# Attention and SwiGLU block: the last exponentials and masks of batch 0, and the order of tile 1's output pieces

## The chip, the core and the metric

The kernel runs on one core of a Trainium2 chip. The core has TensorE (PE, matrix products into PSUM), VectorE (DVE), ScalarE (ACT), GpSimd (POOL) and SyncE (SP); each works through its own instructions in order, and they wait for one another through semaphores. The metric is the device time of one execution in microseconds (us). Seven runs of the kernel before gave 240.5 to 241.52 us, with a median of 241.03 us. One execution was also recorded by the profiler, and all times inside the kernel are of that one, counted from the start of its span.

## What is computed

The reference is an attention with a few global keys and a local window, followed by a gated feed-forward block:

```python
scores = scale * np.matmul(q, k.transpose(0, 1, 3, 2))   # (4, 8, 768, 64): batch, heads, sequence, head width
keep = is_global | is_local            # 8 global keys, a window of 96 keys
bias = -slopes[:, None, None] * dist[None, :, :]
scores = np.where(keep, scores + bias[None], -1e9)
a = np.exp(scores - max); a = a / (sum(a) + 1e-9)
attn = np.matmul(a, v)                 # to rows of 512: heads side by side
g = x @ w_gate                         # 512 -> 1536
out = ((g * sigmoid(g)) * (x @ w_val)) @ w_out      # 1536 -> 512
```

There are 3072 rows (4 batches of 768) and the output is 3072 x 512 in float32.

## The kernel before

**Tiles.** The rows are cut into 8 tiles of 384. Tiles 0 and 1 are the two halves of batch 0, tiles 2 and 3 those of batch 1, and so on. The feed-forward of a tile `t` runs over 12 blocks `f` of 128 hidden columns. A block is a gate product `gps` and a value product `vps` (line 560, 4 matmuls of 384 columns each, in one PSUM bank each); then a tanh on ScalarE (`th`, line 571), and on VectorE `sl` (line 576, reads `th` and the gate bank) and `hT` (line 580, reads the value bank and `sl`). A gate bank comes free when `sl` is done, a value bank when `hT` is.

**Banks.** PSUM has 8 banks here: four that rotate for the attention (`a0` to `a3`), three that rotate for the products (`x0` to `x2`), and `o0`. In the blocks spoken of here, gate 7, value 7 and gate 8 of tile 0 take the three product banks in turn, and gate 9 takes that of gate 7 again. From `late_widen` until `narrow` (block 2 of tile 1) the products rotate over seven banks.

**Output pieces.** The output of 128 rows of a tile is a sum over the 12 blocks of the hidden layer, cut into 4 pieces of 3 matmuls (`out_part`, line 592, 512 columns), here called piece 0 to piece 3. All pieces add into the one bank `o0`; after piece 3 ScalarE copies it out (`osb`, line 598) and SyncE's queue stores it, and piece 0 of the next 128 rows can't begin before that copy is done. Pieces 0 to 3 read the four parts of the output weights `wo` (3 blocks each), which GpSimd's queue loads one after another.

**Attention of batch 0.** The heads go in four pairs. For the second half of batch 0 (rows of tile 1), `sch(hp)` issues the scores of pair `hp` in two parts, called which 0 and which 1. A part needs an `exps` (two activations on ScalarE, line 367) and a `mask` (multiplications by a table on VectorE, line 373: two for part 0, one of 864 columns for part 1). `vas(0, 1)` then sums the denominators (`den`) and the weighted values (`num`) of all pairs on TensorE (line 452). The denominators of the second four heads read part 1 of pair 3 near their end. After that VectorE inverts and spreads the denominators and writes the rows of tile 1 (`xT`).

**Order.** The order on every engine is the order of the program text. Work put off is appended to the list `later`, and `run_later(n)` takes the next n from it. The list `tile0` gives the order for tile 0: a pair `(f, 0)` is the gate of block f with its tanh and `sl`, `(f, 1)` the value with its `hT`. Ahead of most items one step of `later` is taken. The list `stretches` gives for each block of the later tiles how many output pieces follow it (`n_out`), with one step of `later` ahead of each piece; the attention steps of batch 1 are hung on blocks of tile 1 (`first(1, 1)`: transposes after blocks 2 and 5, scores after 4, 6 and 8, values after 9 and inside 10). `outs` is the list of all pieces in order; its first 12 are those of tile 0's three groups of 128 rows.

Before the change, pair 3's `later` holds exps of part 1, mask of part 0, mask of part 1, in this order. Nothing is taken ahead of `(7, 0)`; the exponentials are taken ahead of `(7, 1)`, the first mask ahead of `(8, 0)` and the second ahead of `(9, 0)`. Of tile 0's output pieces, two are issued at the end of `tile0`; tile 1's blocks 0 to 11 are followed by 0, 0, 0, 1, 2, 2, 1, 1, 1, 0, 2, 2.

Of the kernel before, what the change touches and what calls it, by code (L numbers as in the profile page):

```python
# [37 lines left out]
def kernel(  # L38
# [193 lines left out]
    def bank(name, dt=FP32):  # L232
        tag = state["tags"][state["n"] % len(state["tags"])]
        state["n"] += 1
        return single(name, tag, dt)

    def banks(name, dt=FP32):
        return [bank(name, dt) for _ in range(2)]
# [16 lines left out]
    def run_later(n):  # L255
        for _ in range(n):
            if later:
                later.pop(0)()
# [306 lines left out]
    def gate_or_val(t, f, which, c0=0):  # L565
        products(t, f, which, c0, NC)
        dst = gv.pop((f, which))

        if which == 0:
            th = sb2.tile([128, TB], FP32, name="th", tag="th")  # L570
            nc.scalar.activation(out=th, in_=dst[:, 0:TB], func=AF.Tanh, scale=0.5)  # L571
            if t == 0 and f < 4:
                sl = sb2.tile([128, TB], FP32, name="sl", tag="ns", bufs=4)
            else:
                sl = sb2.tile([128, TB], FP32, name="sl", tag="sl", bufs=3)
            nc.vector.scalar_tensor_tensor(  # L576
                out=sl, in0=th, scalar=1.0, in1=dst[:, 0:TB], op0=AluOp.add, op1=AluOp.mult)
            gv["sl", f] = sl
        else:
            nc.vector.tensor_mul(hTs[t][:, f, :], dst[:, 0:TB], gv.pop(("sl", f)))  # L580
# [143 lines left out]
    def sc(b, *units):  # L724
        def step():
            for i, (hp, bk, *other) in enumerate(units):
                pair = pairs[b + 1 if other else b, hp]
                on_vector = pair.b < 2 or bk < 2 or hp % 2 == 0
                exps, mask = pair.scores(
                    bk, nc.vector if on_vector else nc.gpsimd,  # L730
                    [spare("sc") for _ in range(2)] if i == 0 and len(units) == 3
                    else banks("sc"))
                if i == 0:
                    exps()
                else:
                    later.append(exps)
                later.append(mask)
        return step

    def va(b, g, half):  # L740
        return lambda: quads[b, g].values(half, bank, nc.vector)

    def vas(b, half):
        return lambda: both_values(b, half)

    def tr(b, hp):
        return pairs[b, hp].transposes
# [15 lines left out]
    def sch(hp):  # L763
        def step():
            p = pairs[0, hp]
            for which in range(2):
                p.scores_half(1, which, banks("sc"), which == 1 and hp != 1, True)
            if hp != 1:
                later.insert(0, later.pop(1))
        return step  # L770

# [8 lines left out]
    def first(t, b):  # L780
        return {(t, 2): [tr(b, 0), tr(b, 1)],
                (t, 4): [sc(b, (0, 0), (0, 1), (1, 0))],
                (t, 5): [tr(b, 2), tr(b, 3)],
                (t, 6): [sc(b, (1, 1), (2, 0), (2, 1))],
                (t, 8): [sc(b, (3, 0), (3, 1))],
                (t, 9): [va(b, 0, 0)],
                (t, 10, 1): [va(b, 1, 0), lambda: run_later(len(later))]}

    def both(t, b):

        n = b + 1
        return {(t, 0): [sc(b, (0, 2), (1, 2), (2, 2)), fetch(n, 0, 1)],
                (t, 5): [sc(b, (3, 2), (0, 0, n), (1, 0, n)), fetch(n, 2, 3)],
                (t, 8): [vas(b, 1)],
                (t + 1, 0): [sc(n, (0, 1), (1, 1), (2, 0))],
                (t + 1, 4): [sc(n, (2, 1), (3, 0), (3, 1))],
                (t + 1, 8): [vas(n, 0)]}
# [24 lines left out]
    def out_next():  # L822
# [3 lines left out]
             bias_of(0, 0), bias_of(0, 1), scores_of(0), (0, 1), (1, 1), (2, 1),  # L826
             trh(2, 3, False), sch(1), (3, 1), (4, 0), (5, 0), sch(2), (6, 0), (4, 1), (5, 1),
             (6, 1), sch(3), (7, 0), (7, 1), (8, 0), (9, 0), vas(0, 1), late_widen, (10, 0), (8, 1),
             (11, 0), (9, 1), (10, 1), out_next, (11, 1), out_next]

    def ff(t, f0, f1, n_out=(0,)):
        return [(t, f, n_out[(f - f0) % len(n_out)]) for f in range(f0, f1)]

    stretches = [
        (ff(1, 0, 6, (0, 0, 0, 1, 2, 2)) + ff(1, 6, 10, (1, 1, 1, 0)) + ff(1, 10, 12, (2,)), first(1, 1)),
        (ff(2, 0, 12, (1,)) + ff(3, 0, 12, (1,)), both(2, 1)),
        (ff(4, 0, 12, (1,)) + ff(5, 0, 12, (1,)), both(4, 2)),
        (ff(6, 0, 12, (1,)), second(6, 3)),
# [48 lines left out]
    for item in tile0:  # L887
        if callable(item):
            if item is not late_widen and item is not out_next:
                run_later(len(later))  # L890
            item()
            continue
        f, which = item
        if item == (8, 1):
            run_later(3)
        elif item not in ((6, 0), (7, 0)):
            run_later(1)
        gate_or_val(0, f, which, (NC if f < 4 else 0, 2 if f < 2 else 0)[which])
        for fn in after.pop((0, f, which), []):
            fn()  # L900
# [61 lines left out]
```

## Time and profile before

| | |
|---|---|
| median of 7 runs | 241.03 us |
| the profiled execution | 240.69 us |
| its span, first instruction to last | 238.8 us |
| VectorE busy | 170.0 us (71%) |
| ScalarE busy | 127.5 us (53%) |
| GpSimd busy | 94.1 us (39%) |
| granted TensorE clock, mean | 0.998 |

The span is the stretch that the trace covers; 1.89 us of the profiled execution lie outside it. The busy time of TensorE is a union of modelled spans: a matmul of 384 columns shows about 326 ns from start to end, while in an undisturbed row the next one starts 162.5 ns after it. So waits of TensorE are read from start to start, against 162.5 ns after a matmul of 384 columns and 216 ns after one of 512. Between about 50 us and the end, no such step in the trace is longer than its neighbours by more than the 0.05 to 0.1 us that come with a change of the kind of matmul.

### The profile page before, as it was taken

Reading aid. Unit: us, or ns where it says so; the run is one execution under the profiler, and the core shown is the slowest. Engines: PE = TensorE matmul, PEld = TensorE weight load, DVE = VectorE, ACT = ScalarE, POOL = GpSimd, SP = SyncE. Lnnn points to the kernel's source line nnn. Section 1 sums busy time; section 2 is a strip of 40 time slices with the busy share of each in tenths; the row PEclk is TensorE's granted clock in tenths of the full one; section 3 lists DMA queues with packets and bytes.
Section 4 is the critical chain, followed back from the end, with each engine's and each line's share of the span. In section 5 each row is a group of like instructions: output and inputs, shape, how many; then the busy total and the mean of one; then the engine's idle time right before and its main releaser. Section 6 shows DMA issues by size and latency. Waiting matters only on the chain.

```text
span 238.8 us, 6012 instructions
## 1 busy us (share of the span) xinstructions
PE 231.9 (97%) x2406; PEld 133.9 (56%) x2406; DVE 170.0 (71%) x372; ACT 127.5 (53%) x290; POOL 94.1 (39%) x113
## 2 busy tenths in 40 slices
PE   7899989989999999999999999999999999999994
PEld 4565565646555556555655556555655566555543
DVE  6879989948896678675885668676785668555530
ACT  4887774668847275367346365367356535233311
POOL 8976565578960003994082063700032213000000
PEclk9999999999999999999999999999999999999999
DMA  6999999999999447999039449920110110111022
GB/s 133 164 199 200 188 197 204 196 168 164 157 131 143 110 113 91 125 139 124 31 60 113 113 111 132 128 54 6 40 47 0 47 44 3 45 47 44 7 83 88
DMA packets 83332, 25.00 MB, mean 105 GB/s; under 512 B 72600, under 2 KB 80360, under 8 KB 83304
## 3 DMA queue, kind: packets, MB, share of 16 engines
q0 software_dynamic: 64208, 14.05, 66.2%
q1 hardware_dynamic: 18664, 10.36, 17.5%
q8 instruction: 19, 0.31, 0.5%
q10 hardware_dynamic: 432, 0.21, 0.4%
q14 instruction: 9, 0.07, 0.1%
HBM read 28.62 MB, written 6.29 MB: 146 GB/s over the span
## 4 chain that ended last, share of the span: by engine, by line
PE 91%; DVE 3%; DMA 2%; POOL 1%; ACT 1%; issue 1%; DVEq 0%; ACTq 0%; POOLq 0%
PE gps L560 26%; PE vps L560 26%; PE ops L592 25%; PE num L452 4%; PE sc L392 3%; DMA q<-in_q_dram 2%; PE den L452 2%; PE trs L272 1%; PE ops L608 1%; DVE sl L576 1%; PE sc L356 1%; PE sc L345 1%; POOL k L118 1%; DVE xT L510 1%; ACT th L571 1%; PE trs L298 1%
## 5 line engine op out<-in xcount | busy, mean ns | idle before, releaser
L571 ACT ACTIVATE th<-gps 128x384 f32<-128x384 f32 x96 | 47.3, 494 | 60.9 <-PE gps L560 56.5
L560 PE MATMUL gps<-xT,wg 128*128 128x384 f16 x384 | 77.8, 327 | 0.3 <-DVE xT L510 0.3
L576 DVE SCALAR_TENSOR_TENSOR sl<-th,gps 128x384 f32<-128x384 f32 x96 | 52.6, 551 | 35.6 <-ACT th L571 34.8
L560 PE MATMUL vps<-xT,wv 128*128 128x384 f16 x384 | 77.6, 326 | 0.0
L592 PE MATMUL ops<-wo,hT 128*128 128x512 f16 x276 | 73.1, 379 | 0.7 <-ACT osb L598 0.7
L580 DVE TENSOR_TENSOR hT<-vps,sl 128x384 f16<-128x384 f32 x96 | 52.8, 553 | 7.5 <-PE vps L560 0.2
L560 PEld LDWEIGHTS <-wg 128*128 128x128 f16 x384 | 35.4, 98 | 31.6 <-issue 2.2
L560 PEld LDWEIGHTS <-wv 128*128 128x128 f16 x384 | 37.2, 98 | 25.5 <-DMA wv<-in_moe_w_val_dram 0.3
L592 PEld LDWEIGHTS <-hT 128*128 128x128 f16 x276 | 26.9, 98 | 24.8 <-issue 1.2
L400 ACT ACTIVATE at<-sc 128x432 f16<-128x432 f32 x72 | 33.8, 534 | 11.0 <-PE sc L392 11.0
L529 POOL TENSOR_TENSOR xT<-ns,rb 128x384 f16<-128x384 f32 x10 | 9.8, 996 | 65.1 <-ACT ns L525 33.8
L169 POOL DMA_DIRECT2D vS<-in_v_dram x28 | 24.7, 892 | 5.4 <-DMA kst<-in_k_dram 1.6
L598 ACT ACTIVATE osb<-ops 128x512 f32<-128x512 f32 x23 | 13.7, 597 | 15.1 <-PE ops L592 14.9
L411 DVE TENSOR_TENSOR at<-at,masks 128x864 f16<-128x864 f16 x20 | 12.2, 609 | 7.1 <-ACT at L400 7.1
L411 POOL TENSOR_TENSOR at<-at,masks 128x864 f16<-128x864 f16 x4 | 7.3, 1821 | 23.9 <-ACT at L400 19.3
L525 ACT COPY ns<-num 128x384 f32<-128x384 f32 x24 | 9.8, 494 | 10.8 <-PE num L452 10.8
L192 POOL DMA_DIRECT2D kst<-in_k_dram x16 | 14.1, 896 | 1.8 <-PE sc L392 1.3
L192 POOL DMA_DIRECT2D qst<-in_q_dram x16 | 13.7, 880 | 0.7 <-issue 0.5
L367 ACT ACTIVATE at<-sc 128x432 f16<-128x432 f32 (+2 forms) x32 | 11.5, 461 | 1.7 <-PE sc L356 1.7
L408 DVE TENSOR_TENSOR at<-at,masks 128x432 f16<-128x432 f16 x24 | 8.1, 377 | 4.4 <-ACT at L400 4.4
L452 PE MATMUL num<-at,vS 128*32 128x216 f16 (+6 forms) x576 | 11.0, 224 | 0.0
L462 DVE STREAM_TRANSPOSE dT<-den 128x384 f32<-128x384 f32 x16 | 9.3, 580 | 1.1 <-PE den L452 0.4
(72 smaller groups left out, 166.0 us busy)
## 6 DMA issues: line engine op xcount, KB each, us to landing
out_dram<-osb SPq DMA_DIRECT2D x23, 256.0 KB
vS<-in_v_dram POOLq DMA_DIRECT2D x24, 120.0 KB, 5.6
wg<-in_moe_w_gate_dram POOLq DMA_DIRECT2D x6, 256.0 KB, 8.9
wv<-in_moe_w_val_dram POOLq DMA_DIRECT2D x6, 256.0 KB, 8.0
wo<-in_moe_w_out_dram POOLq DMA_DIRECT2D x4, 384.0 KB, 11.2
qst<-in_q_dram POOLq DMA_DIRECT2D x16, 96.0 KB, 4.7
kst<-in_k_dram POOLq DMA_DIRECT2D x16, 90.0 KB, 4.5
kst<-in_k_dram POOLq DMA_DIRECT2D x2, 384.0 KB, 11.7
```

What stands on the lines that cost most here:

```text
L169: nc.gpsimd.dma_start(out=vSs[b][NG:NG + n, c, :, :], in_=v[b, :, KC * c:KC * c + n, :].rearrange("h p d -> p h d"))
L192: nc.gpsimd.dma_start(out=st[b][p0:p0 + n, h // 2, :, h % 2, :], in_=src[b, h, 0:n * J].rearrange("(t p) d -> p t d", p=n))
L367: nc.scalar.activation(out=at[:, hi, 0:col + n], in_=sc[hi][:, 0:col + n], func=AF.Exp, scale=scale)
L400: nc.scalar.activation(out=at[:, hi, :], in_=sc[hi][:, 0:BANK], func=AF.Exp, scale=scale)
L411: mul_eng.tensor_mul(at, at, m[:, :, o:o + BANK])
L452: nc.tensor.matmul(dst[r, o:o + n], lhsT=ones[:, 0:32] if side is None else vals[:, 4 * g + j, side::2], rhs=pairs[b, 2 * g + j // 2].at[c ...
L560: nc.tensor.matmul(gv[f, which][:, 0:TB], lhsT=w[:, c, 128 * f:128 * f + 128], rhs=x_of(t)[:, c, :], start=(c == 0), stop=(c == NC - 1))
L571: nc.scalar.activation(out=th, in_=dst[:, 0:TB], func=AF.Tanh, scale=0.5)
L576: nc.vector.scalar_tensor_tensor(out=sl, in0=th, scalar=1.0, in1=dst[:, 0:TB], op0=AluOp.add, op1=AluOp.mult)
L580: nc.vector.tensor_mul(hTs[t][:, f, :], dst[:, 0:TB], gv.pop(("sl", f)))
L592: nc.tensor.matmul(ops, lhsT=hTs[t][:, f, 128 * i:128 * i + 128], rhs=wo[:, f, :], start=(f == 0), stop=(f == NFF - 1))
L598: nc.scalar.mul(out=osb, in_=ops, mul=0.5)
```

## The change

```diff
@@ sch(hp) @@
             for which in range(2):
-                p.scores_half(1, which, banks("sc"), which == 1 and hp != 1, True)
-            if hp != 1:
+                p.scores_half(1, which, banks("sc"), which == 1 and hp == 2, True)
+            if hp == 2:
                 later.insert(0, later.pop(1))
@@ tile0 @@
-             (11, 0), (9, 1), (10, 1), out_next, (11, 1), out_next]
+             (11, 0), (9, 1), (10, 1), out_next, (11, 1)]
@@ stretches @@
-        (ff(1, 0, 6, (0, 0, 0, 1, 2, 2)) + ff(1, 6, 10, (1, 1, 1, 0)) + ff(1, 10, 12, (2,)), first(1, 1)),
+        (ff(1, 0, 6, (1, 0, 0, 1, 1, 2)) + ff(1, 6, 10, (1,)) + ff(1, 10, 12, (2,)), first(1, 1)),
@@ loop over tile0 @@
         if item == (8, 1):
             run_later(3)
-        elif item not in ((6, 0), (7, 0)):
+        elif item != (6, 0):
             run_later(1)
```

With it, pair 3's exponentials of part 1 are issued at once behind those of part 0, ahead of the tanh of block 7; its mask of part 0 is taken ahead of `(7, 0)` and its mask of part 1 ahead of `(7, 1)`. Pairs 1 and 2 keep their order. Of the two pieces at the end of `tile0` the second is issued after block 0 of tile 1; one of the two after block 4 moves back, so that block 4 has one, and block 9 has one where it had none. Tile 1's blocks are followed by 1, 0, 0, 1, 1, 2, 1, 1, 1, 1, 2, 2. The sum of pieces from the end of `tile0` to block 11 is 14 in both, and from block 10 on each place has the same piece as before. No instruction is added or removed, and nothing computed is changed.

## The prediction

> **What bounds the kernel.** TensorE does. I read the page's busy line first, then the waits from 29 us on with TensorE alone, then the chain of waits, and last the timelines of the three engines around each place, with the starts of single instructions.
>
> ```profile
> PE 231.9 (97%) x2406; PEld 133.9 (56%) x2406; DVE 170.0 (71%) x372; ACT 127.5 (53%) x290; POOL 94.1 (39%) x113
> ```
> ```profile
> PE ops L592 <- ACT osb L598: 0.7, 1, 0.7
> PE den L452 <- DVE at L373: 0.6, 1, 0.6
> ```
>
> Two waits are left, both where the change works. From start to start they are longer than the view says, since it counts from a modelled end. In the denominators one matmul starts at 31.885 and the next at 32.762; such neighbours follow within 0.003, so **0.874 us** are lost. Between piece 3 and piece 0 in block 4 of tile 1 the starts are 48.800 and 49.865, against 0.216: **0.849 us**. The same reading finds a third that no view names: value 11 to piece 1 of tile 0, 38.680 to 39.009 against 0.1625: **0.167 us**. Its weights were being loaded:
>
> ```profile
> 38.68 0.10 PEld L592 LDWEIGHTS <-hT 128*128 128x128 f16 x1
> 39.01 0.81 PE L592 MATMUL ops<-wo,hT 128*128 128x512 f16 x3
> 39.25 0.75 POOL L151 DMA_DIRECT2D qst<-in_q_dram  x1 [1.42 <-DMA wo<-in_moe_w_out_dram]
> ```
>
> The hT weights were in at 38.68, and a GpSimd issue at 39.25 had waited for a wo load. Elsewhere such issues start about 0.28 after the landing that frees them (qst landed 42.52, issue 42.815), so wo's second part landed near 38.97.
>
> **Part 1, exponentials and masks.** The queues now (timelines, 28 to 33 us):
>
> ```profile
> 28.63 0.67 ACT L367 ACTIVATE at<-sc 128x264 f16<-128x264 f32 x2 [0.97 <-PE sc L356]
> 29.58 0.49 ACT L571 ACTIVATE th<-gps 128x384 f32<-128x384 f32 x1 [0.28 <-PE gps L560]
> 29.96 0.95 ACT L367 ACTIVATE at<-sc 128x432 f16<-128x432 f32 x2
> ...
> 30.10 0.55 DVE L576 SCALAR_TENSOR_TENSOR sl<-th,gps 128x384 f32<-128x384 f32 x1 [0.37 <-ACT th L571]
> 30.76 0.56 DVE L580 TENSOR_TENSOR hT<-vps,sl 128x384 f16<-128x384 f32 x1
> 31.23 0.49 DVE L373 TENSOR_TENSOR at<-at,masks 128x144 f16<-128x144 f16 x2
> 31.64 0.54 DVE L576 SCALAR_TENSOR_TENSOR sl<-th,gps 128x384 f32<-128x384 f32 x1
> 32.11 0.60 DVE L373 TENSOR_TENSOR at<-at,masks 128x864 f16<-128x864 f16 x1
> ```
>
> The last mask ends at 32.708 and the denominators go on 0.054 later. The price of moving it is at gate 9. That gate reuses gate 7's bank, and sl 7 ends at 30.654, gate 9 starts at 30.709: this bank is already the last to come, with nothing to spare.
> - ScalarE: the second short exponential starts at 28.917 and takes 0.287 to the next start (28.630 to 28.917). The two long ones, whose scores are in PSUM by 28.785, start at 29.204 and 29.614 (0.410 apart, as 29.965 and 30.375). Tanh 7 follows at 30.024 instead of 29.578: 0.446 late, ending 30.515.
> - VectorE: sl 7 starts 0.032 after it (30.069 to 30.101), 30.547 to 31.100. Gate 9 starts 0.055 later, 31.155: **0.446 late**.
> - The masks: the first is in the gap before sl 7, behind hT 6 (start 29.179 plus 0.47). The second starts 0.464 after sl 7 (as 31.644 to 32.108), at 31.01, its exponentials done at 30.15. It ends at 31.61, so TensorE may read at 31.67. The denominators reach it at 31.888 + 0.446 = 32.33: no wait, 0.67 to spare.
>
> So 0.874 is freed and 0.446 paid: **0.428 us** gained. hT 7, sl 8, sl 9 then start at 31.53, 32.01, 32.53 (before: 30.76, 31.64, 32.63). hT 7 and sl 8 free product banks for the last values, which reach them at 33.07 and 33.37: hidden. VectorE's chain to xT is only 0.10 earlier, while TensorE is 0.43 earlier.
>
> A rule against moving masks: the Trainium skill, "SBUF — State Buffer", section "Who interferes with whom", says a VectorE operation with two SBUF inputs contends with a GpSimd one that reads SBUF, and whichever started first holds the port to its end. GpSimd issues the second wo load from 29.50 to 30.26 and a kst load from 30.58 to 31.36, where the masks will be. If it held for DMA issues, the second mask would wait until 31.36 and end at 31.96, still hidden, and the first, held to 30.26, would push sl 7 from 30.55 to 30.67: gain 0.31 instead of 0.43. But here a mask begun at 28.663 under a wo issue (28.06 to 28.81) took 0.596, against 0.600 free of one. I take nothing.
>
> **Part 2, piece 1 leaves the end of tile 0.** The wait of 0.167 goes: behind value (1, 0) it stands near 39.7, past 38.97. Tile 1's first gate comes earlier by 0.428 + 0.167 + 0.648 (three matmuls of 0.216): 39.654 becomes 38.41. It needs xT, whose last write ends at 38.464 − 0.10 = 38.36, and only its fourth matmul, at 38.90, reads that. About 0.5 to spare. If xT came later, each us would cost one. After piece 1, TensorE is ahead by **0.595**. The loads do not move with it: queries of pairs 0 and 1 landed 42.52, read at 43.41; wo's third part 45.02, read at 45.83; its fourth 46.83, read at 47.77. All hidden; the least margin is 0.84.
>
> **Part 3, block 4.** With one piece, the copy of `o0` (0.597) lies under the scores, block 5 and so on; the 0.849 goes. What is late next? Everything reused close behind. Scores of batch 1 start at 50.605 − 0.595 − 0.849 − 0.648 = 48.51; their second bank is that of gate 4, free at 48.995 − 0.595 + 0.055 = 48.46. Gate 5 at 49.17 needs hT 4, 49.657 − 0.595 + 0.055 = 49.12. The first exponential queues behind the copy (48.62, plus 0.494 to the next start as at 57.586): it ends at 49.64 and value 5 wants its bank at 49.83. Margins of 0.05, 0.05 and 0.14: I cost them at nothing; from below, zero is the floor, and from above 0.1 in all if a latency is a little longer.
>
> Block 7 now has piece 3 and its copy on ScalarE between the exponentials. Tanh 8 is then 0.59 late against TensorE (59.53 with TensorE 2.09 ahead), sl 8 ends near 60.6, and value 9 wants that bank near 61.18: hidden, 0.5 to spare. The next scores want their bank at 60.05, its exponential ends at 59.68. SyncE's queue has the store of that copy behind the copies of global values instead of ahead of them: those go earlier, and no reader is early. Piece 1 in block 9 stands ahead of the values; it returns the 0.648, and its step of `later` issues the last mask no later. Tanh 10, on time behind its gate (64.945 − 1.44, plus 0.86), lets sl 10 start at 64.88 instead of 66.51, where it stood behind masks and inversions; the rest of VectorE's chain to the next xT follows it, 1.6 earlier, and TensorE is 1.44 earlier, so the first gate of tile 2, tight before (xT ends 71.355, its fourth matmul 71.659), is no tighter. From there the order is the old one, without a wait to the end: an advance is kept.
>
> **Sum.** 0.428 + 0.167 + 0.849 = **1.44 us**. Against the profiled execution, 240.69 (span 238.80 and 1.89 around it), that is 239.25, a span of 237.36. This execution lies 0.34 under the median of 241.03, so the median to expect is 239.59, **239.6 us**.
>
> **Rivals.** (a) *Part 1 gives nothing*: tanh 7 late by twice what I count, or a second wait behind gate 9 (sl 8 and sl 9 are queued there), so that the bank wait replaces the mask wait. Against it: 0.446 is two intervals that the trace shows. Time: 241.03 − 0.167 − 0.849 = 240.0. Chance 0.12. (b) *The bank wait outgrows it*: sl 7 is behind tanh 7, and that behind four exponentials. Any delay of this queue stops TensorE at gate 9 one for one, and then xT. At 0.874 it eats part 1, and from 0.446 + 1.44 = 1.89 us the kernel is slower; at 2.4 us, 241.5. For it: this bank has no slack. Against: nothing in the four exponentials waits after 28.8. Chance 0.05. (c) *Loads bind*: were the pairs' queries to land more than 0.84 later than 42.52, the gain is cut, to nothing at 2.3. For it: GpSimd's issues wait for landings. Against: nothing before 42 us on that queue moves. It gives 240.3 at a slip of 1.5. Chance 0.05. The forecast itself: 0.78, with 239.3 to 239.9 around it.
>
> The range, 239.1 to 240.2, reaches to (a) and, below, to gate 9 not being late at all (another 0.45). A measurement of this kernel tells about 0.2%, 0.48 us, from no change. Faster by more than that: the forecast, (a), and 0.02 of (c): 0.92. Within: the rest of (c), 0.03. Slower: (b), 0.05.
>
> **What would show it.** The wait for L373 gone; gate 9 starting 0.5 after its predecessor with sl 7 just before it; piece 1 of tile 0 on pitch; no wait for L598; no new step above 0.1 us after 32 us. It is wrong if gate 9 loses over 0.6, or if TensorE waits at scores, gate 5 or value 5, or at xT.

## The result, and the profile after

The changed kernel takes 239.49 us (median of 12 runs, 239.27 to 240.28) against 241.03 us (31 runs, 240.5 to 241.98). The ratio, estimated over all of these runs, is 0.9943 with a 95% interval from 0.9933 to 0.9953: 1.4 us less, between 1.1 and 1.6. (The two medians alone differ by 1.54 us.) The forecast was 1.44 us and 239.6 us.

The profiled execution of the changed kernel took 240.01 us with a span of 238.15 us, only 0.68 us less than before. Its opening was longer: pair 3's last scores of the second half start at 29.044 us in it and at 28.309 before, and nothing of the change lies ahead of them. In the ten traces of this document these scores start anywhere from 28.19 to 29.97 us. So I measure between two marks, the start of those scores and the start of the last output (line 608): 204.616 us before, 203.210 after, **1.406 us** less.

From the page of the changed kernel, the busy line and the first line of the chain that ended last:

```profile
PE 233.0 (98%) x2406; PEld 135.2 (57%) x2406; DVE 169.6 (71%) x372; ACT 127.7 (54%) x290; POOL 94.1 (40%) x113
PE 95%; DVE 2%; ACT 1%; issue 0%; DVEq 0%; ACTq 0%
```

The waits of TensorE from 28 us on (who waits, for whom, us in total, times, longest). Where before had two rows, the copy of the output bank and the mask, there is one new one:

```profile
PE gps L560 <- DVE sl L576: 0.3, 1, 0.3
```

The chain of waits of the changed kernel in order of time (start, us, what) shows how that row comes about, and that nothing else breaks TensorE's row afterwards:

```profile
29.65 1.23 ACT at L367 x3
30.89 0.39 ACT th L571
31.28 0.02 issue
31.30 0.56 DVE sl L576
31.87 0.04 issue
31.91 0.81 PE gps L560 x4
32.72 0.72 PE den L452 x40
33.44 1.22 PE num L452 x80
34.66 0.76 PE gps L560 x4
35.42 0.73 PE vps L560 x4
...
48.75 0.65 PE ops L592 x3
49.40 0.66 PE sc L392 x12
```

Read it upwards from gate 9 at 31.91: it started when sl 7 ended, sl 7 when tanh 7 ended, and tanh 7 stood behind pair 3's exponentials. The denominators (`x40` in one piece) are not broken any more, and block 4's single output piece is followed at once by the scores. The gate rows of 0.76 each follow a change of the kind of matmul. One more row is longer than its neighbours without that reason: value 8 with 0.73 in place of 0.65. The timeline of VectorE and TensorE says why (start, us, engine, line, operation):

```profile
34.70 0.58 DVE L462 STREAM_TRANSPOSE dT<-den 128x384 f32<-128x384 f32 x1
...
35.33 0.81 PE L560 MATMUL vps<-xT,wv 128*128 128x384 f16 x4
```

The transpose of the second denominators ends at 35.280; value 8, whose bank it frees, starts at 35.333.

Start to start, the time that TensorE loses at each place between the marks, in us:

| | before | change |
|---|---|---|
| gate 9, for the bank of gate 7 | 0.031 | 0.493 |
| denominators, for pair 3's last mask | 0.874 | none |
| value 8, for the bank of the second denominators | none | 0.078 |
| piece 1 of tile 0, for its weights | 0.167 | none |
| block 4, for the copy of the output bank | 0.849 | none |
| value (2, 0), for a bank that an sl frees | 0.052 | none |
| sum | 1.973 | 0.571 |

The sums differ by 1.402 us, the marks by 1.406.

### The profile page after: what moved, and what is told of

It reads as the page before. It is cut to its first block, busy times and chain, and to the rows that moved or that the text cites. A ratio compares the mean times of both kernels' runs of the same rounds, so it can differ in the third digit from the quotient of the medians.

```text
span 238.2 us, 6012 instructions
## 1 busy us (share of the span) xinstructions
PE 233.0 (98%) x2406; PEld 135.2 (57%) x2406; DVE 169.6 (71%) x372; ACT 127.7 (54%) x290; POOL 94.1 (40%) x113
## 4 chain that ended last, share of the span: by engine, by line
PE 95%; DVE 2%; ACT 1%; issue 0%; DVEq 0%; ACTq 0%
PE gps L560 26%; PE vps L560 26%; PE ops L592 25%; PE num L452 4%; PE sc L392 3%; PE den L452 2%; PE trs L298 2%; PE sc L345 2%; PE sc L356 2%; PE trs L272 1%; PE warm L628 1%; PE ops L608 1%; DVE sl L576 1%; DVE xT L510 1%; ACT at L367 1%; ACT th L571 1%
```

## The experiments

Theory: each of these waits is worth its own term, and the price of part 1 is paid through tanh 7, sl 7 and the bank. The rivals are written with each run.

**The exponentials and masks alone.**

```diff
 (against the kernel before)
-                p.scores_half(1, which, banks("sc"), which == 1 and hp != 1, True)
-            if hp != 1:
+                p.scores_half(1, which, banks("sc"), which == 1 and hp == 2, True)
+            if hp == 2:
...
-        elif item not in ((6, 0), (7, 0)):
+        elif item != (6, 0):
```

> Pair 3's exponentials and masks moved up as in the change, the output pieces as before. Theory (two bank waits and one load, each worth its own term): 0.874 us freed in the denominators, 0.46 paid at gate 9, and 0.08 at value 8, which waits for the second inversion; net 0.33 to 0.36 us, ratio about 0.9985. In its trace gate 9 follows gate 8 at about 0.65 us instead of 0.19; block 4's wait of 0.849 stays. Piece 1 of tile 0 comes earlier by 0.35 while its load does not: its wait grows to about 0.5, and the gain of part 1 is lost again at this place (ratio 1.000), if the opening is as fast as in the trace of before; if that wait was for hT 8 on VectorE instead, it moves along with VectorE and the gain is kept. Rival (part 1 pays nothing at gate 9): 0.87 us, ratio 0.9964.

Measured: 240.70 us against 241.03 in the same session, ratio 0.9990, interval 0.9980 to 0.9999; between the marks 0.338 us less. Gate 9 loses 0.496, value 8 0.071, the denominators nothing, block 4 0.848: the terms as expected. Part 1 alone is worth about a third of a us. The times alone hardly tell that from nothing, so it rests on the terms of the trace; the rival's 0.87 is outside the interval. Piece 1 did not behave as I expected: its wait is 0.182, not 0.5. Its timeline tells what it waited for:

```profile
38.51 0.55 DVE L580 TENSOR_TENSOR hT<-vps,sl 128x384 f16<-128x384 f32 x1
38.53 0.10 PEld L592 LDWEIGHTS <-hT 128*128 128x128 f16 x1
38.88 0.81 PE L592 MATMUL ops<-wo,hT 128*128 128x512 f16 x3
39.12 0.75 POOL L151 DMA_DIRECT2D qst<-in_q_dram  x1 [1.37 <-DMA wo<-in_moe_w_out_dram]
```

The second part of wo landed at 38.84 and piece 1 started at 38.877, while hT 8 ended only at 39.06. So it was the load, and not hT 8, as the near ends of both in the trace of before (38.93 for hT 8) could have let one think; piece 1 reads only blocks 3 to 5. The wait did not grow because this execution reached the first mark 0.21 us later and its load landed 0.13 us ahead of the 38.97 estimated for the trace of before.

**The output pieces alone.**

```diff
 (against the changed kernel: back to the old order of pair 3)
-                p.scores_half(1, which, banks("sc"), which == 1 and hp == 2, True)
-            if hp == 2:
+                p.scores_half(1, which, banks("sc"), which == 1 and hp != 1, True)
+            if hp != 1:
...
-        elif item != (6, 0):
+        elif item not in ((6, 0), (7, 0)):
```

> The output pieces of tile 1 spread as in the change, pair 3's exponentials and masks as before. Theory: block 4's 0.849 us and piece 1's 0.167 go, and 0.05 at the start of tile 2: 1.02 to 1.07 us, ratio 0.9956. The wait of 0.874 in the denominators stays in the trace, and gate 9 follows gate 8 without more than 0.04. Rival (the parts are not additive, a wait removed comes back at the scores, gate 5 or value 5 of block 5): under 0.5 us, ratio over 0.998.

Measured: 239.80 us against 241.03, ratio 0.9950 (0.9932 to 0.9967); between the marks 1.057 us less. One row of waits is left:

```profile
PE den L452 <- DVE at L373: 0.6, 1, 0.6
```

The pieces bring three quarters of the gain. With the run before, 0.338 + 1.057 = 1.395 against 1.406 together: the parts add up.

**Blocks 4 and 9 alone.**

```diff
 (against the kernel before)
-        (ff(1, 0, 6, (0, 0, 0, 1, 2, 2)) + ff(1, 6, 10, (1, 1, 1, 0)) + ff(1, 10, 12, (2,)), first(1, 1)),
+        (ff(1, 0, 6, (0, 0, 0, 1, 1, 2)) + ff(1, 6, 10, (1,)) + ff(1, 10, 12, (2,)), first(1, 1)),
```

> Only the pieces behind blocks 4 and 9 of tile 1 moved (both pieces stay at the end of tile 0; exponentials and masks as before). Theory: block 4's 0.849 us goes alone, with 0.05 at the start of tile 2, while the denominators' 0.874 and piece 1's 0.1 to 0.2 stay: 0.85 to 0.90 us, ratio 0.9963. Rival (the copy of the output bank comes back as a wait at the scores, gate 5, value 5 or value 9): under 0.6 us, and a new step over 0.1 us in the trace there.

Measured: 240.02 us against 240.92 in the same session, ratio 0.9961 (0.9948 to 0.9975), 0.9 us. Between the marks it is 1.046 us less, more than this edit can give. The difference is piece 1, which still stands at the end of tile 0 here and yet lost nothing: this execution's opening was late by 1.67 us, for a load of the value weights (chain of waits, start, us, what),

```profile
10.78 9.47 DMA wv<-in_moe_w_val_dram
20.26 0.05 issue
20.30 0.82 PE vps L560 x4
```

so the output weights were there in time. The 0.849 of block 4 is one of the schedule, in every execution; the 0.167 of piece 1 is a race between the opening and a load, and is not always there to be gained. No new step came at the scores, gate 5, value 5 or value 9.

**Tanh 7 ahead of the second exponentials.** These and the second mask are taken together ahead of value 7, everything else as in the change.

```diff
 (against the changed kernel)
-                p.scores_half(1, which, banks("sc"), which == 1 and hp == 2, True)
+                p.scores_half(1, which, banks("sc"), which == 1 and hp != 1, True)
...
+        elif item == (7, 1):
+            run_later(2)
         elif item != (6, 0):
```

> The change, but tanh 7 stays ahead of pair 3's second exponentials; these and the second mask are taken ahead of value 7. Theory: gate 9's wait goes (0.46 us back), the mask still ends at about 31.55 on the clock of before, ahead of the denominators' need at 31.89, so no wait there; but value 8 then reaches its bank 0.4 us before the second inversion frees it, and most of the 0.46 is lost there again. 0.1 to 0.2 us faster than the change, ratio to before about 0.9937. Rival (gate 9's wait is not tanh 7's): gate 9 still loses 0.46, time as with the change, 0.9943.

Measured: 239.32 us against 241.03, ratio 0.9923 (0.9904 to 0.9942); between the marks 1.553 us less than before, 0.147 less than with the change. The timeline of the three engines:

```profile
29.45 0.49 ACT L571 ACTIVATE th<-gps 128x384 f32<-128x384 f32 x1 [0.28 <-PE gps L560]
29.84 0.95 ACT L367 ACTIVATE at<-sc 128x432 f16<-128x432 f32 x2
29.91 1.49 PE L560 MATMUL gps<-xT,wg 128*128 128x384 f16 x8
30.82 0.61 DVE L373 TENSOR_TENSOR at<-at,masks 128x864 f16<-128x864 f16 x1 [0.29 <-ACT at L367]
31.32 0.79 PE L452 MATMUL den<-at,ones 128*32 128x72 f16 x40
...
33.18 0.33 PEld L452 LDWEIGHTS <-vS 128*32 128x32 f16 x19 [0.24 <-issue]
```

Gates 8 and 9 are one row (`x8`), and the 40 denominators are one row: gate 9's wait was tanh 7's, and the mask can come early enough without it. The 0.46 us come back only in part. I expected the loss at value 8, for 0.4; it is 0.066 there, because TensorE first lost about 0.3 in the middle of the numerators, at 32.862 to 33.179, on an instruction that waits for no semaphore. That place is taken up below.

**The change with other banks.** The seven-bank rotation begins with the banks of the first numerators, which ScalarE copies out early; the attention's own rotation continues at the bank of value 9.

```diff
 (against the changed kernel)
-        state["x"] = ([state["tags"][(state["n"] + i) % 4] for i in range(4)]
+        state["x"] = ([state["tags"][(state["n"] + i + 2) % 4] for i in range(4)]
...
-        state["n"] += 3
+        state["n"] += 1
```

> The change, with the seven-bank rotation beginning at the banks of the first numerators, and the attention's rotation continued at the bank of value 9 after it. Theory (value 8 waits for the second inversion to free its bank): the step of 0.078 at value 8 goes and nothing else changes, 0.08 us faster than the change between the last scores of pair 3 and the last output. Rival (value 8 waits for something else on VectorE or for its weights): the step stays.

Measured: 239.41 us against 240.92, ratio 0.9937 (0.9921 to 0.9953); between the marks 0.067 us less than with the change, and no step at value 8. The difference is too small for the times; the trace shows the bank to be the cause.

**Both, and what binds next.** First tanh 7 ahead with the rotated banks only (without the second line of the last diff):

> As the run with tanh 7 first, and the seven-bank rotation after the values of tile 1 begins with the two banks of the first numerators, which ScalarE copies out early, and not with those of the denominators, which wait for VectorE. Theory: value 8's wait goes too, so 0.9 us are gained at this place and 1.9 in all, less up to 0.14 that piece 0 may wait for its weights (landed 36.73, wanted near 36.65): 1.8 to 2.0 us, ratio 0.992. Rival (VectorE's chain to tile 1's rows binds next): gate (1, 0) waits for xT, no faster than the change, 0.9943.

Measured: 239.32 us against 241.03, ratio 0.9931 (0.9912 to 0.9951); between the marks 1.483 us less than before. That is a miss: I expected 1.8 to 2.0. Value 8's wait went and xT did not bind, but 0.18 us were lost again inside the numerators, and the rotation now gave the first transposes of batch 1 the bank of value (1, 1), which VectorE frees late:

```profile
42.70 0.56 DVE L580 TENSOR_TENSOR hT<-vps,sl 128x384 f16<-128x384 f32 x1
...
43.31 0.53 PE L272 MATMUL trs<-ident,kst 128*64 128x128 f16 x12 [0.17 <-DVE hT L580]
```

From start to start this costs 0.24 us. With the second line, which gives them an earlier bank:

> Tanh 7 first, the rotated banks, and the attention's rotation continued so that the first transposes of batch 1 get the bank of value (1, 0) and not that of value (1, 1). Theory: no wait at gate 9, the denominators, value 8 or the transposes; the step of 0.2 to 0.3 us inside the last numerators, which waits for no semaphore, stays. Between the last scores of pair 3 and the last output 1.7 us shorter than before, 0.3 shorter than with the change; ratio 0.993. Rival (loads bind: the queries land near 42.5): a step at the transposes stays, no gain over 1.5.

Measured: 239.30 us against 240.92, ratio 0.9948 (0.9930 to 0.9966); between the marks 1.736 us less than before, as expected, but not by the account I gave. Of the step in the numerators only 0.04 was left, and instead the third matmul of value 8 waited 0.145: it is the first to read the last part of the value weights, which landed at 35.76, and it started at 35.807. The transposes do not wait. Loads bind there, not at the queries as the rival had it.

**The step inside the numerators.** The same kernel with the warming matmuls at the start cut finer: 72 more instructions on TensorE ahead of all others, in about the same time.

```diff
 (against the run before)
-            nc.tensor.matmul(warm[:, 0:256], lhsT=ones[:, 0:128], rhs=ones[:, 0:256],
+            nc.tensor.matmul(warm[:, 0:64], lhsT=ones[:, 0:128], rhs=ones[:, 0:64],
...
-    fill(12)
+    fill(48)
```

> As the run before, with the warming matmuls at the start cut into 48 of 64 columns in place of 12 of 256: about the same time, 72 more instructions on TensorE ahead of everything. Theory (the step inside the numerators is TensorE waiting for its own instructions, which come in blocks of a fixed number): the step leaves the 102nd of the 120 denominator and numerator matmuls and is found some 36 matmuls earlier, or not at all. Rival (a value or a bank arrives late): it stays at the 102nd.

Measured: 239.05 us against 240.92, ratio 0.9934 (0.9918 to 0.9950); between the marks 1.795 us less than before. There is no such step at the 102nd matmul, nor 36 matmuls earlier. Two short waits are left: gate 9 loses 0.074, behind sl 7 (ended 30.932, gate 9 at 30.985), and value 8's third matmul 0.093, again 0.05 after a landing (34.70, 34.749). Between the marks this is 0.39 us shorter than the change and the shortest of all, but the intervals of the two overlap (the change: 0.9933 to 0.9953), so the times do not show it to be faster.

## Why the prediction was right, point by point

- **The mask wait of 0.874 us** goes as a whole, as forecast. The last mask ends at 32.374, and TensorE reaches the denominators that need it near 33.09.
- **Gate 9.** Forecast: 0.446 later than before, on top of the 0.031 it lost already. Measured: 0.493 against 0.477. The four exponentials and tanh 7 start at 29.366, 29.654, 29.925, 30.336 and 30.746, intervals of 0.288, 0.271, 0.411 and 0.410 where the sum had 0.287, 0.287, 0.410 and 0.410. Tanh 7 itself took 0.523 where the sum had 0.491; less the 0.016 by which the second interval was shorter, that is the 0.016 missed. Among its signs the prediction has gate 9 "0.5 after its predecessor": by its own sum that is the loss, and the starts lie 0.656 apart. That sl 7 and its bank carry the delay is shown by the run with tanh 7 ahead.
- **What is late next.** The step "VectorE's chain to xT is only 0.10 earlier, while TensorE is 0.43 earlier" was right in the main (counted from the first mark, measured 0.07 for the last write of xT and 0.43 for gate 10), but it was followed only to the first gate of tile 1. Value 8 reads nothing of that chain and still needs it: its bank is the second denominators'. That is 0.078 us that the sum lacks; both runs with other banks show it.
- **Piece 1.** The wait went. In the changed kernel the weights landed at 38.34, ahead of the piece's old place as well as of its new one, and the run with blocks 4 and 9 alone shows a piece in the old place that lost nothing. So the term is right for the two traces' difference only where the opening is as quick as in the trace of before; in the changed kernel's execution the wait would not have come even with the piece in its old place. That the sum came out right here is in part luck.
- **The loads behind it.** The least margin that the prediction lists is 0.81 us, of the third part of wo (45.02 to 45.83), and not the 0.84 it names. Nothing hung on it: in the changed kernel the three loads landed 1.9 to 2.2 us ahead of their first readers.
- **Block 4.** The 0.849 went, and the three tight places behind it (scores, gate 5, value 5, with margins of 0.05 to 0.14) held: the scores start at 49.334, the bank they need is free by 49.27.
- **The first gate of tile 2.** It was called no tighter than before. A step of 0.052 behind it, where value (2, 0) had waited for a bank, went as well; the sum had not counted it.
- **The rule on the shared port.** The second mask began at 31.773 inside an issue of GpSimd (a query load from 31.40 to 32.14) and took 0.601 us, as against 0.600 and 0.596 before. Five masks of 864 columns lie in this trace almost wholly under such issues and took 0.596 to 0.601; the 16 that met none have a median of 0.604. Nothing was lost to it, as the row of the old trace had said.

The terms missed, minus 0.078 and minus 0.016 on one side and plus 0.052 on the other, nearly cancel, and that too is luck: 1.444 forecast, 1.406 measured between the marks. Rival (a), that part 1 pays nothing, is refuted by its own run (0.338 us); (b) had its mechanism right and its size wrong, since gate 9 is late by 0.46 and not by 1.9; (c) did not happen, though loads do bind once the other waits are gone.

## What to carry to other kernels

A wait is measured from start to start; the view of waits counted 0.6 and 0.7 us where 0.87 and 0.85 were to be had. When work is moved ahead on an in-order engine, look at what it overtakes: here the tanh that it overtook was already the last to free a bank, and half of the gain was paid there. When TensorE gets ahead of another engine by some tenths, every bank that this engine still frees is the next candidate, not only the data that it produces.

## What the runs showed of the hardware that I had not expected

**TensorE can wait for its own instructions.** In the first two kernels with tanh 7 ahead, the step in the numerators comes at the same instruction, the 102nd of the 120 matmuls of line 452. It waits for no semaphore, and the load of its stationary operand is delayed with it ("issue" in the timeline). The trace's instruction queue fetches 16,384 bytes for TensorE 19 times, on average every 250 of its recorded instructions. The fetch before that place began at 30.89, 31.02 and 31.77 us in the first three kernels with tanh 7 ahead, and TensorE went on 2.29, 2.42 and 2.49 us later; in the kernel before, the change and the runs of its parts it came there 2.7 us or more after the fetch and did not wait. With 72 instructions put in front, the fetch fell at 26.09 and the step was gone. The Trainium skill, "Runtime: NRT & Kernel Launch", section "Instruction fetch mechanics", says that instructions are refilled in blocks of 256 and that crossing a block is mostly hidden. These runs agree with the size and show some 0.04 to 0.3 us where small matmuls run through a block in little more than 2 us. That the fetch is the cause is argued from these times and from the one run with shifted instructions; no run stretched the fetch alone. One thing does not fit a plain wait for the data: each of the three fetches took about 0.95 us, so its bytes had landed 1.3 to 1.6 us before TensorE went on. What fills that time, no trace here shows.

**The opening runs at two rates.** In the trace of before, the bias products of 432 columns start 0.333 us apart at 4.4 us and 0.193 apart from 7.4 us on. In the changed kernel's trace a second pair, at 7.6 us, is still 0.335 apart, and the next, at 10.7 us, 0.193. The page's row of the granted clock reads 9 in every slice of both, but time without a record counts there as full speed. The trace's own records of the granted clock begin at 5.84 us in the trace of before and at 10.51 us in the changed kernel's, and the rate changes there. It does so in all ten traces, whose records begin between 4.03 and 10.51 us: up to 13 us, the pairs ahead of the first record are 0.333 to 0.335 apart, one that lies across it 0.266, and those behind it 0.192 to 0.194, except two (0.238 and 0.277). What sets this moment was not tried. It does not set the time of the first mark: with the records from 4.03 us on, the run of the pieces alone reached that mark at 28.57, and the kernel before, with 5.84, at 28.31. These ten openings differ by up to 1.8 us, more than the change is worth, so two single spans of this kernel tell little unless the opening is left out.
